# A first load in halves, and divisions and spreads moved to later slots, in a kernel of two attentions

## The chip, the cores and the metric

The kernel runs on one core of a Trainium2 chip. The metric is the device time in microseconds (us) of one execution. The core has five engines that run side by side, each through its own stream of instructions in order: PE (matrix products), DVE (element-wise work), ACT (functions such as exp, and copies), POOL (masks) and SP, which here issues every DMA. They wait for one another only through semaphores. Products land in PSUM banks; everything else lies in SBUF or in DRAM.

## The reference

Two attentions over 2048 tokens, width 640, 32 heads of 20, on their own inputs and weights; the outputs are put side by side. A is causal attention within chunks of 512 tokens, mixed by a gate with a read from a memory that the earlier chunks have filled. B is causal attention over a sliding window of 256 tokens.

```
# A, for each chunk s of 4
p = softmax(qs @ ks.T * scale + causal)
num, den = phi(qs) @ M, phi(qs) @ z + 1e-6       # phi(t) = t + 1 if t > 0 else exp(t)
o = g * num / den + (1 - g) * (p @ vs)           # g = sigmoid(beta), one per head
M, z = M + phi(ks).T @ vs, z + phi(ks).sum()
# B
p = softmax(where(0 <= i - j < 256, q @ k.T * scale, -1e9))
o = p @ v
# both
out = o @ wo
```

## The kernel before

The work is cut into eight phases, B and A in turn for chunks 0 to 3 of 512 tokens. A phase has eight units of four heads. The score blocks of a phase are packed, so that a pack fills 512 columns for each of four heads; phases have 20 packs (B's first and all of A's) or 24. A pack is a **slot**: 172 slots in all, numbered from 0. In a slot, `body` (lines 656 to 717) issues in this order:

1. whatever an earlier slot has put off to the start of this one (`self.after`, filled by `at`);
2. `scores` of the pack (line 451): the score products on PE, then two exponentials on ACT (line 465, each over two heads) and masks on POOL (lines 479 and 485);
3. what was put off to follow the scores (`self.behind`, filled by `at_end`), such as the parts of phi;
4. `weigh` of a unit whose exponentials are two slots old (line 495): the weighted sums on PE, a cast to the tile `oc` on DVE (line 527), and a DMA transpose to the tile `ocT` (line 529);
5. `prefetch`: turns of finished token tiles (DMA transposes to `oT`, line 571), as long as fewer than three are open;
6. projections, updates and reads of A's memory, and output products, chosen by `pick` from lists with estimated costs.

A unit's sums carry the sum of its weights as one more column. `normalise` (lines 540 to 564) divides: a reciprocal (line 544) and a product (line 549) on DVE, out of `ocT` into the token tile `ot`; where it is the last unit of a chunk of A other than the first and last, it also adds the memory's read (line 561). `weigh` puts `normalise` off by four slots (three in A's last chunk). When a chunk's eighth unit is divided, its four token tiles are ready to be turned and multiplied by the output weights (`out_half`, line 574).

The queries and keys of chunk 0 of B are projected straight into the layout that the scores need, four heads at partitions 0, 32, 64 and 96 (`proj_padded`, line 237). All others go through `proj` (line 261): the product is cast to a tile `qk` (line 270), written to a DRAM scratch `qd` or `kd` (line 271), and read back from there by `spread` (line 280) into `qp` and `kp`, in four DMAs, one for each place of a head. `proj` puts a spread off by two slots; it waits in SP's stream until the writes have landed, with everything that is queued on SP behind it.

PSUM has three two-bank tiles named `Sc`, for the scores, and two one-bank tiles named `D`, for all other products; a `D` tile is free again when DVE (or ACT) has copied it out. PE's stream is in order, so a product without a free `D` tile holds back all scores behind it.

The start: one DMA loads the first 512 tokens of B into a tile that bears the name `omem` (line 125), ahead of the weights on SP. Ten products of a zero tile run meanwhile on PE (line 210). Then `first_x` turns the tokens on PE, 20 transposes of 128x128 for five slices of the width (line 216), two slices to a `Sc` tile, and copies each slice to `xTB`, on DVE for the even slices (line 219) and on ACT for the odd ones (line 221).

Of the kernel before, what the change touches and what calls it, by code (L numbers as in the profile page):

```python
# [9 lines left out]
BF16 = mybir.dt.bfloat16  # L10
F32 = mybir.dt.float32

P = 128
S = 2048
D = 640
# [4 lines left out]
KT = 5  # L20
NC = 4
CH = 512
CT = CH // P
# [59 lines left out]
class Kern:  # L83
# [21 lines left out]
    def load_x(self, br, c):  # L105
        t = self.io.tile([P, KT, CH], BF16, name="xT" + br, bufs=1)
        self.nc.sync.dma_start_transpose(out=t[:], in_=self.x[br][c * CH:(c + 1) * CH, :])
        self.xT[br] = t

    def load_w(self, name, ap, eng, pad=0, halves=None):  # L110
        n = ap.shape[1]
# [7 lines left out]
    def setup(self):  # L119
        nc, cp, ins = self.nc, self.cp, self.ins  # L120
        wB = ins["B_wqkv"]
        self.w, self.wt = {}, {}
        brow = cp.tile([P, H], BF16, name="brow")
        xs = self.io.tile([P, CT, D], BF16, name="omem", bufs=1)
        nc.sync.dma_start(out=xs[:], in_=self.x["B"][0:CH, :].rearrange("(t p) d -> p t d", p=P))
        wk, wq = wB[:, D:2 * D], wB[:, 0:D]
        self.load_w("Bk", wk, nc.sync, 32, 0)
        self.load_w("Bq", wq, nc.sync, 32, 0)
        self.load_w("Bk", wk, nc.sync, 32, 1)
        self.load_w("Bq", wq, nc.sync, 32, 1)  # L130
        self.load_w("Bv", wB[:, 2 * D:3 * D], nc.sync)
        nc.sync.dma_start(out=brow[:], in_=ins["A_beta"].partition_broadcast(P))
        self.load_x("A", 0)
        self.load_w("Ak", ins["A_wk"], nc.sync)
        self.load_w("Aq", ins["A_wq"], nc.sync)
        self.load_w("Av", ins["A_wv"], nc.sync)
        self.load_w("Bo", ins["B_wo"], nc.sync)
        self.load_w("Ao", ins["A_wo"], nc.sync)

        z = self.wk.tile([P, CH], BF16, name="oc", bufs=2)  # L140
        nc.vector.memset(z[:], 0.0)
        one = cp.tile([P, 1], F32, name="one")
# [25 lines left out]
        self.v, self.vt = vs, vt  # L168
        self.first_x(xs, z)

        bm = cp.tile([P, KT, 8], F32, name="bmask")
        nc.gpsimd.memset(bm[:], 1.0)
        for m in range(KT):
            off = P * m - DH * (P * m // DH)
            nc.gpsimd.affine_select(out=bm[:, m, :], in_=bm[:, m, :], pattern=[[-DH, 8]],
                                    compare_op=ALU.is_ge, fill=0.0, base=off,
                                    channel_multiplier=1)
            nc.gpsimd.affine_select(out=bm[:, m, :], in_=bm[:, m, :], pattern=[[DH, 8]],
                                    compare_op=ALU.is_ge, fill=0.0, base=DH - 1 - off,
                                    channel_multiplier=-1)  # L180
        self.bm = bm
        self.macc = cp.tile([P, KT, 8, DH + 1], F32, name="macc")
        self.gate(brow)
# [20 lines left out]
    def first_x(self, xs, z):  # L204

        nc = self.nc
        for _ in range(2):
            ps = self.dtile([P, CH], F32)
            for i in range(5):
                nc.tensor.matmul(ps[:], lhsT=z[:, 0:P], rhs=z[:], start=(i == 0), stop=(i == 4))  # L210
        t = self.io.tile([P, KT, CH], BF16, name="xTB", bufs=1)
        for kt in range(KT):
            if kt % 2 == 0:
                ps = self.ps.tile([P, 2, 2 * CH], BF16, name="Sc", bufs=3)
            for tt in range(CT):
                nc.tensor.transpose(out=ps[:, kt % 2, tt * P:(tt + 1) * P],
                                    in_=xs[:, tt, kt * P:(kt + 1) * P], identity=self.ident[:])
            if kt % 2 == 0:
                nc.vector.tensor_copy(out=t[:, kt, :], in_=ps[:, 0, 0:CH])
            else:  # L220
                nc.scalar.copy(out=t[:, kt, :], in_=ps[:, 1, 0:CH])
        self.xT["B"] = t

# [13 lines left out]
    def proj_padded(self, which, g):  # L237

        nc = self.nc
        if g == 0:  # L240
            t = self.io.tile([P, G, CH], BF16, name="%spB" % which,
                             bufs=2 if which == "k" else 1)
            if which == "q":
                self.qp["B"] = t
            else:
                self.kp["B", 0] = t
        t = self.qp["B"] if which == "q" else self.kp["B", 0]
        ps = self.dtile([P, CH], F32)
        w = self.wt["B" + which]
        for kt in range(KT):  # L250
            for j in range(4):
                c0 = kt * D + DH * (4 * g + j)
                nc.tensor.matmul(ps[32 * j:32 * j + 32, :], lhsT=w[:, c0:c0 + 32],  # L253
                                 rhs=self.xT["B"][:, kt, :], start=(kt == 0),
                                 stop=(kt == KT - 1), tile_position=(0, 32 * j))
        if g == 0 and which == "q":
            nc.scalar.copy(out=t[:, g, :], in_=ps[:])
        else:
            nc.vector.tensor_copy(out=t[:, g, :], in_=ps[:])

    def proj(self, br, c, which, m, st):
        nc = self.nc
        if m == 0:
            st[which] = self.dram.tile([KT * P, CH], BF16, name="%sd%s" % (which, br), bufs=2)
        ps = self.dtile([P, CH], F32)
        for kt in range(KT):
            nc.tensor.matmul(ps[:], lhsT=self.w[br + which][:, kt, m * P:(m + 1) * P],  # L267
                             rhs=self.xT[br][:, kt, :], start=(kt == 0), stop=(kt == KT - 1))
        t = self.wk.tile([P, CH], BF16, name="qk", bufs=4)
        nc.vector.tensor_copy(out=t[:], in_=ps[:])  # L270
        nc.sync.dma_start(out=st[which][m * P:(m + 1) * P, :], in_=t[:])
        cut = {1: (0, 3), 3: (3, 6), 4: (6, 8)} if (br, c) in (("A", 0), ("B", 1)) else {4: (0, 8)}
        if (br, c) == ("A", 1):
            cut = {2: (0, 4), 4: (4, 8)}
        if m in cut:
            self.at(self.slot + 2, lambda: self.spread(br, c, which, st, *cut[m]))
        if br == "A":
            self.phi(c, which, m, t, st)

# [42 lines left out]
    def vproj(self, br, c, tt, hf):  # L322
        nc = self.nc
        ps = self.dtile([P, CH], F32)
        for kt in range(KT):
            nc.tensor.matmul(ps[:, 0:320], lhsT=self.xT[br][:, kt, tt * P:(tt + 1) * P],  # L326
                             rhs=self.w[br + "v"][:, kt, hf * 320:(hf + 1) * 320],
                             start=(kt == 0), stop=(kt == KT - 1))
        src = ps[:, 0:320].rearrange("p (h e) -> p h e", e=DH)
# [3 lines left out]
        else:  # L333
            nc.vector.tensor_tensor(  # L334
                out=self.v["A"][0][:, tt, hs, 0:DH], in0=src,
# [159 lines left out]
    def weigh(self, u):  # L495
        nc = self.nc
# [13 lines left out]
        for n, (kt, off, q0, nq, pt) in enumerate(jobs):  # L510
            v = self.vt[u.br][(kt // CT) % 2 if u.br == "B" else 0]
            for j in range(4):
                v0 = VW * (4 * u.g + j)
                nc.tensor.matmul(O[32 * j:32 * j + 32, q0 * P:(q0 + nq) * P],  # L514
                                 lhsT=v[:, kt % CT, v0:v0 + 32],
                                 rhs=pt[:, j, off * P:(off + nq) * P],
# [10 lines left out]
        nc.vector.tensor_copy(out=oc[:], in_=O[:])  # L527
        tp = self.wk.tile([P, CT, P], BF16, name="ocT", bufs=4)
        nc.sync.dma_start_transpose(out=tp[:], in_=oc[:])
        late = 3 if u.br == "A" and u.c == NC - 1 else 4  # L530
        self.at(self.slot + late, lambda: self.normalise(u, tp))

    def turn_here(self, u, oc):
# [285 lines left out]
```

## Time and profile before

| | us |
|---|---|
| median of three runs | 392.62 |
| lowest and highest run | 392.05, 395.66 |
| the profiled execution, as timed | 390.19 |
| its span in the profile | 388.1 |

| engine | busy us | share of the span | instructions |
|---|---|---|---|
| PE | 340.4 | 88% | 4060 |
| ACT | 338.1 | 87% | 384 |
| DVE | 276.7 | 71% | 581 |
| POOL | 251.8 | 65% | 392 |

The span runs from the first to the last instruction that the profile shows; 2.1 us of the time lie outside it. The granted clock of PE was 0.991 of full speed on average. The exponentials of line 465 are 320.7 of ACT's busy time, 344 of them.

Rows of a timeline give, in this order, the start in us from the span's start, the time taken, the engine, the line, the operation, the tile written and the tile read, and how many instructions are merged in the row; in brackets stands how long the engine was idle before it, and what ended that. SPq is SP's queue of DMA issues: its times are those of issuing, and the data land later. The trace also has an event for each landing. Rows of waits give who waited for whom, the total in us, how many times, and the longest.

### The profile page before, as it was taken

What the parts mean: (1) busy time and instruction counts of PE and PEld (TensorE: products, weight loads), DVE (VectorE), ACT (ScalarE), POOL (GpSimd) and SP (SyncE); (2) the same over time, 40 slices, a digit from 0 to 9 for tenths busy, and PEclk for the clock granted to TensorE, in tenths of its full rate; (3) what the DMA queues carried; (4) which work ended last, traced back from release to release, by engine and by line L of the source; (5) the groups of instructions that cost most, each with busy time, mean ns of one, the idle gap of its engine ahead of it and who ended that gap; (6) DMA issues with size and microseconds to landing.
All of it is one profiled execution on the core that took longest, in us unless ns stands there. A gap on an engine that the chain in (4) does not pass through costs nothing.

```text
span 388.1 us, 10554 instructions
## 1 busy us (share of the span) xinstructions
PE 340.4 (88%) x4060; PEld 161.3 (42%) x4060; DVE 276.7 (71%) x581; ACT 338.1 (87%) x384; POOL 251.8 (65%) x392
## 2 busy tenths in 40 slices
PE   7999988977998798988997989898999989988884
PEld 3433434322443344444543335444454435544442
DVE  2467667634788868788778886789877887777583
ACT  2867789985999889888999999988999999999972
POOL 9657564542777587635578888844458988955550
PEclk9999999998999989999999999999999999999999
DMA  8993328647434597728575697758474377736312
GB/s 256 314 285 77 47 83 151 113 105 187 134 80 134 143 173 141 135 71 137 117 135 135 127 190 126 149 104 110 116 146 120 92 169 129 113 78 113 96 30 70
DMA packets 110738, 50.77 MB, mean 131 GB/s; under 512 B 81760, under 2 KB 110688, under 8 KB 110688
## 3 DMA queue, kind: packets, MB, share of 16 engines
q1 hardware_dynamic: 110688, 50.10, 61.1%
q8 instruction: 32, 0.52, 0.6%
q14 instruction: 18, 0.15, 0.1%
HBM read 16.39 MB, written 14.42 MB: 79 GB/s over the span
## 4 chain that ended last, share of the span: by engine, by line
PE 42%; ACT 24%; DVE 16%; issue 6%; POOL 6%; DMA 3%; SPq 0%; POOLq 0%; DVEq 0%; ACTq 0%
ACT pt L465 22%; PE D L267 13%; PE Sc L459 7%; PE D L326 6%; PE D L580 5%; PE D L514 5%; PE D L253 4%; POOL pt L479 3%; DVE qk L270 3%; POOL pt L485 3%; DVE oc L527 3%; ACT pe L310 2%; PE Sc L628 2%; DVE omem L445 1%; DMA ocT<-oc 1%
## 5 line engine op out<-in xcount | busy, mean ns | idle before, releaser
L465 ACT ACTIVATE pt<-Sc 128x1024 bf16<-128x1024 f32 (+1 forms) x344 | 320.7, 1077 | 32.3 <-PE Sc L459 28.2
L479 POOL TENSOR_SCALAR_AFFINE_SELECT pt<-pt 128x512 bf16<-128x512 bf16 x254 | 167.6, 671 | 117.2 <-ACT pt L465 116.9
L485 POOL TENSOR_SCALAR_AFFINE_SELECT pt<-pt 128x512 bf16<-128x512 bf16 x112 | 78.6, 717 | 5.1 <-ACT pt L465 4.8
L270 DVE CAST qk<-D 128x512 bf16<-128x512 f32 x70 | 47.9, 687 | 29.4 <-PE D L267 26.8
L527 DVE CAST oc<-D 128x512 bf16<-128x512 f32 x62 | 42.7, 688 | 19.9 <-PE D L514 19.8
L459 PE MATMUL Sc<-qpB,kpB 20*128 20x256 bf16 (+2 forms) x704 | 43.3, 277 | 7.8 <-ACT pt L465 4.7
L459 PE MATMUL Sc<-qpA,kpA 20*128 20x384 bf16 (+3 forms) x512 | 41.0, 302 | 5.8 <-ACT pt L465 5.0
L580 PEld LDWEIGHTS <-oT 128*128 128x128 bf16 x280 | 25.4, 98 | 17.9 <-issue 6.6
L583 DVE CAST ot<-D 128x320 bf16<-128x320 f32 x56 | 27.0, 485 | 7.2 <-PE D L580 6.4
L459 PEld LDWEIGHTS <-kpB 20*128 20x128 bf16 x704 | 13.6, 92 | 42.5 <-issue 38.5
L267 PE MATMUL D<-xTA,Aq 128*128 128x512 bf16 x100 | 24.9, 379 | 4.6 <-DVE oc L527 3.5
L326 PE MATMUL D<-Av,xTA 128*128 128x320 bf16 x160 | 26.2, 300 | 2.8 <-DVE vA L334 1.6
L514 PE MATMUL D<-pt,vA 128*32 128x256 bf16 (+3 forms) x576 | 23.5, 287 | 5.7 <-DVE qk L270 2.2
L580 PE MATMUL D<-Bo,oT 128*128 128x320 bf16 x160 | 27.3, 306 | 1.0 <-DVE omem L445 0.4
L267 PE MATMUL D<-xTA,Ak 128*128 128x512 bf16 x100 | 25.3, 384 | 2.1 <-DVE qk L270 2.0
L326 PE MATMUL D<-Bv,xTB 128*128 128x320 bf16 x160 | 26.0, 300 | 1.4 <-DVE oc L527 0.9
L514 PE MATMUL D<-pt,vB 128*32 128x384 bf16 (+2 forms) x720 | 26.1, 277 | 0.5 <-DVE qk L270 0.3
L459 PEld LDWEIGHTS <-kpA 20*128 20x128 bf16 x512 | 11.7, 91 | 30.6 <-issue 27.9
L267 PE MATMUL D<-xTB,Bq 128*128 128x512 bf16 x75 | 19.8, 396 | 3.4 <-DVE qk L270 3.2
L549 DVE TENSOR_TENSOR otB<-ocT,rr 128x320 bf16<-128x320 bf16 x32 | 20.2, 631 | 1.1
L544 DVE RECIPROCAL rr<-ocT 128x16 f32<-128x16 bf16 x62 | 15.1, 243 | 8.0 <-DMA ocT<-oc 8.0
L580 PE MATMUL D<-Ao,oT 128*128 128x320 bf16 x120 | 20.1, 299 | 0.7 <-DVE qk L270 0.4
(84 smaller groups left out, 358.8 us busy)
## 6 DMA issues: line engine op xcount, KB each, us to landing
out_dram<-ot SPq DMA_DIRECT2D x31, 160.0 KB
kdA<-qk SPq DMA_DIRECT2D x20, 128.0 KB
qdA<-qk SPq DMA_DIRECT2D x20, 128.0 KB
kdB<-qk SPq DMA_DIRECT2D x15, 128.0 KB
qdB<-qk SPq DMA_DIRECT2D x15, 128.0 KB
kpB<-kdB SPq DMA_DIRECT2D x8, 160.0 KB
qpB<-qdB SPq DMA_DIRECT2D x8, 160.0 KB
kpA<-kdA SPq DMA_DIRECT2D x8, 160.0 KB
```

Of the source, the lines that this page charges most:

```text
L267: nc.tensor.matmul(ps[:], lhsT=self.w[br + which][:, kt, m * P:(m + 1) * P], rhs=self.xT[br][:, kt, :], start=(kt == 0), stop=(kt == KT - 1))
L270: nc.vector.tensor_copy(out=t[:], in_=ps[:])
L326: nc.tensor.matmul(ps[:, 0:320], lhsT=self.xT[br][:, kt, tt * P:(tt + 1) * P], rhs=self.w[br + "v"][:, kt, hf * 320:(hf + 1) * 320], start ...
L459: nc.tensor.matmul(ps[j // 2][:, j % 2, off * P:(off + nq) * P], lhsT=kp[rows, u.g, k0:k0 + P], rhs=self.qp[u.br][rows, u.g, q0 * P:(q0 + ...
L465: nc.scalar.activation(out=pt[:, 2 * hp:2 * hp + 2, 0:pk.used], in_=ps[hp][:, :, 0:pk.used], func=ACT.Exp, scale=SCALE)
L479: nc.gpsimd.affine_select(out=blk, in_=blk, pattern=[[0, 4], [1, P]], compare_op=ALU.is_ge, fill=0.0, base=0, channel_multiplier=-1)
L485: nc.gpsimd.affine_select(out=blk, in_=blk, pattern=[[0, 4], [-1, P]], compare_op=ALU.is_ge, fill=0.0, base=-1, channel_multiplier=1)
L514: nc.tensor.matmul(O[32 * j:32 * j + 32, q0 * P:(q0 + nq) * P], lhsT=v[:, kt % CT, v0:v0 + 32], rhs=pt[:, j, off * P:(off + nq) * P], star ...
L527: nc.vector.tensor_copy(out=oc[:], in_=O[:])
L549: nc.vector.tensor_tensor(out=o[:, :, cols].rearrange("p b (j e) -> p b j e", j=4), in0=pv[:, :, :, 0:DH], in1=rr[:].unsqueeze(3).to_broad ...
L580: nc.tensor.matmul(ps[:, 0:320], lhsT=st["oT"][:, m, :], rhs=self.w[br + "o"][:, m, hf * 320:(hf + 1) * 320], start=(m == 0), stop=(m == K ...
L583: nc.vector.tensor_copy(out=st["ot"][:, hf * 320:(hf + 1) * 320], in_=ps[:, 0:320])
```

## The change

Five things are different. Slices of the turned tokens are now a list, so that they may lie in two tiles. The first 512 tokens of B come in two DMAs of 256 tokens each, into tiles that bear the names `otA` and `otB`. There are seven products of zeros in place of ten, and the five turned slices go to five PSUM tiles of their own (three `Sc`, two `D`); all transposes of the first half stand ahead of those of the second, and a slice is copied after its second half, the odd ones into a tile that bears the name `phiq`. The spreads of chunks 2 and 3 are put off by three slots in place of two. `normalise` is put off by six slots in chunks 0 and 1 and by five in chunks 2 and 3, in place of four; A's last chunk keeps its three.

```diff
@@ load_x
-        self.xT[br] = t
+        self.xT[br] = [t[:, kt, :] for kt in range(KT)]
@@ setup
-        xs = self.io.tile([P, CT, D], BF16, name="omem", bufs=1)
-        nc.sync.dma_start(out=xs[:], in_=self.x["B"][0:CH, :].rearrange("(t p) d -> p t d", p=P))
+        xs = [self.io.tile([P, CT, D], BF16, name="ot" + br, bufs=2) for br in "AB"]
+        for i in range(2):
+            nc.sync.dma_start(out=xs[i][:, 0:2, :], in_=self.x["B"][256 * i:256 * i + 256, :]
+                              .rearrange("(t p) d -> p t d", p=P))
@@ first_x
-        for _ in range(2):
+        for n in (4, 3):
             ps = self.dtile([P, CH], F32)
-            for i in range(5):
-                nc.tensor.matmul(ps[:], lhsT=z[:, 0:P], rhs=z[:], start=(i == 0), stop=(i == 4))
-        t = self.io.tile([P, KT, CH], BF16, name="xTB", bufs=1)
-        for kt in range(KT):
-            if kt % 2 == 0:
-                ps = self.ps.tile([P, 2, 2 * CH], BF16, name="Sc", bufs=3)
-            for tt in range(CT):
-                nc.tensor.transpose(out=ps[:, kt % 2, tt * P:(tt + 1) * P],
-                                    in_=xs[:, tt, kt * P:(kt + 1) * P], identity=self.ident[:])
-            if kt % 2 == 0:
-                nc.vector.tensor_copy(out=t[:, kt, :], in_=ps[:, 0, 0:CH])
-            else:
-                nc.scalar.copy(out=t[:, kt, :], in_=ps[:, 1, 0:CH])
-        self.xT["B"] = t
+            for i in range(n):
+                nc.tensor.matmul(ps[:], lhsT=z[:, 0:P], rhs=z[:], start=(i == 0), stop=(i == n - 1))
+        ps = [self.ps.tile([P, 4 * CH], BF16, name="Sc", bufs=3) for _ in range(3)]
+        ps += [self.dtile([P, 2 * CH], BF16) for _ in range(2)]
+        t = [self.io.tile([P, KT, CH], BF16, name=n, bufs=1) for n in ("xTB", "phiq")]
+        self.xT["B"] = [t[kt % 2][:, kt, :] for kt in range(KT)]
+        for i in range(2):
+            for kt in range(KT):
+                for tt in range(2):
+                    c0 = (2 * i + tt) * P
+                    nc.tensor.transpose(out=ps[kt][:, c0:c0 + P],
+                                        in_=xs[i][:, tt, kt * P:(kt + 1) * P],
+                                        identity=self.ident[:])
+                if i and kt % 2 == 0:
+                    nc.vector.tensor_copy(out=self.xT["B"][kt], in_=ps[kt][:, 0:CH])
+                elif i:
+                    nc.scalar.copy(out=self.xT["B"][kt], in_=ps[kt][:, 0:CH])
@@ proj
-            self.at(self.slot + 2, lambda: self.spread(br, c, which, st, *cut[m]))
+            self.at(self.slot + (3 if c > 1 else 2), lambda: self.spread(br, c, which, st, *cut[m]))
@@ weigh
-        late = 3 if u.br == "A" and u.c == NC - 1 else 4
+        late = 3 if u.br == "A" and u.c == NC - 1 else 6 if u.c < 2 else 5
```

Left out are the places in `proj_padded`, `proj` and `vproj` that take a slice from the list in place of the tile. In `proj`, `c` is the chunk that is projected, one ahead of the phase's own.

More of the change, by code (lines that the diff above doesn't have):

```diff
@@ L253, in proj_padded @@
                 nc.tensor.matmul(ps[32 * j:32 * j + 32, :], lhsT=w[:, c0:c0 + 32],
-                                 rhs=self.xT["B"][:, kt, :], start=(kt == 0),
+                                 rhs=self.xT["B"][kt], start=(kt == 0),
                                  stop=(kt == KT - 1), tile_position=(0, 32 * j))
@@ L267, in proj @@
             nc.tensor.matmul(ps[:], lhsT=self.w[br + which][:, kt, m * P:(m + 1) * P],
[L268 removed]
+                             rhs=self.xT[br][kt], start=(kt == 0), stop=(kt == KT - 1))
         t = self.wk.tile([P, CH], BF16, name="qk", bufs=4)
@@ L325, in vproj @@
         for kt in range(KT):
-            nc.tensor.matmul(ps[:, 0:320], lhsT=self.xT[br][:, kt, tt * P:(tt + 1) * P],
+            nc.tensor.matmul(ps[:, 0:320], lhsT=self.xT[br][kt][:, tt * P:(tt + 1) * P],
                              rhs=self.w[br + "v"][:, kt, hf * 320:(hf + 1) * 320],
```

## Prediction

> **What bounds the kernel now.** I read the page first, then the waits, then the timelines of ACT, DVE and SP's queue, and last the chain of waits at the start and around 100 us. The page says that ACT (338.1 us of 388.1) and PE (340.4) are both busy for most of the span. The program runs in 172 slots, each with two exponentials of line 465 on ACT; counting those rows in pairs gives each slot's start. Where nothing else interferes a slot takes 1.81 us, and 1.81 us is two such exponentials, so there ACT is the bound. The rest is lost where ACT waits:
>
> ```profile
> ACT pt L465 <- PE Sc L459: 28.2, 36, 3.9
> DVE rr L544 <- DMA ocT<-oc: 8.0, 6, 3.3
> ```
>
> These are totals, times and the longest. The second row is the wait the change aims at: a division (line 544) that stands in DVE's stream before its turned tile ocT has landed. The two longest of its six, and what ACT did beside them:
>
> ```profile
> 79.77 0.25 DVE L544 RECIPROCAL rr<-ocT 128x16 f32<-128x16 bf16 x1 [2.74 <-DMA ocT<-oc]
> ...
> 87.97 0.25 DVE L544 RECIPROCAL rr<-ocT 128x16 f32<-128x16 bf16 x1 [3.31 <-DMA ocT<-oc]
> ```
>
> ```profile
> 71.59 9.44 ACT L465 ACTIVATE pt<-Sc 128x1024 bf16<-128x1024 f32 x10
> 82.87 5.61 ACT L465 ACTIVATE pt<-Sc 128x1024 bf16<-128x1024 f32 x6 [1.84 <-PE Sc L459]
> 92.38 2.85 ACT L465 ACTIVATE pt<-Sc 128x1024 bf16<-128x1024 f32 x3 [3.91 <-PE Sc L459]
> ```
>
> DVE stands still, no D bank is emptied, PE stops, and ACT idles 1.84 + 3.91 = 5.75 us (slots 32 and 35). Why is ocT late? SP's queue there is an almost solid row of issues from 56.99 to 96.15; a few of its rows:
>
> ```profile
> 71.72 3.84 SPq L571 DMA_TRANSPOSE oT<-otB  x3
> 76.09 1.14 SPq L271 DMA_DIRECT2D kdA<-qk  x1
> 77.34 1.20 SPq L529 DMA_TRANSPOSE ocT<-oc  x1
> 79.29 1.41 SPq L291 DMA_DIRECT2D kpA<-kdA  x4
> ...
> 83.99 1.41 SPq L291 DMA_DIRECT2D qpA<-qdA  x4
> 85.50 2.50 SPq L529 DMA_TRANSPOSE ocT<-oc  x2
> ...
> 97.45 1.42 SPq L291 DMA_DIRECT2D qpB<-qdB  x4
> ```
>
> The ocT issued at 77.34 was ready in oc at 70.4 (cast 69.72 + 0.69): SP is some 7 us behind the engines. That matters for what follows, because SP also carries the next phase's q (qpB, 97.45), which slot 40 needs.
>
> **The change, part by part.** The after kernel keeps every projection, score, weighted sum and output product in its slot. What moves: the division two slots later in chunks 0 and 1, one later in chunks 2 and 3 (A's last chunk unchanged); the turns (line 571) that hang on a finished tile: B0's first three from slot 25 to 27, A0's first from 46 to 47, B3's first from 157 to 158; spreads of chunks 2 and 3 one slot later; and the start.
>
> *Start.* The chain there is one load, then turning in shared tiles:
>
> ```profile
> 0.80 4.26 DMA omem<-in_B_x_dram
> 5.11 0.41 PE Sc L216 x4
> 5.54 0.43 DVE xTB L219
> ...
> 7.14 0.61 PE Sc L216 x8
> 7.75 2.30 PE D L253 x40
> ```
>
> From landing (5.06) to the first projection takes 2.62 us (the timeline puts it at 7.68), because PE waits for a copy before reusing each shared tile. After: the first half lands earlier and its 10 transposes (10 x 0.076, from 8 in 0.61) run before the second lands. The second half ends the same bytes in the same queue; it lands between 5.06 and 5.57 (one more issue, 0.49 to 0.51), I take 5.2. Then ACT, which must empty the bank that the first projection takes over, copies at 5.2 + 0.05 + 4 x 0.076 + 0.05 = 5.6 and needs 2 x 0.58 = 1.16, to 6.8; DVE's three copies (3 x 0.42 + gaps) end at 6.75. The projection starts at 6.8 in place of 7.68: -0.9. Its weights landed at 6.54 by the trace's landing events, so they still cover this. The PE has three matmuls less to warm up: the rows of line 210 step by 0.43 us until 3.79 and faster after, so seven end near 4.25, and ten transposes follow at once. Bounds: -1.0 (landing at 5.06) and +0.3 (landing at 5.57 and 20 transposes at double their 0.076 plus a projection stretched by 0.6). Nothing holds the gain up behind it: the next weights, Bv, land at 12.20 and are wanted at 13.70 - 0.9.
>
> The Trainium skill, "TensorE: Matmul & The Clock Gate", Part 1, speaks against this edit: the warm-up is about 3.4 us of activity, not a number of matmuls. This trace's cadence turned faster about 2.9 us after the first matmul, so the rule's window is near what seven matmuls fill. By the rule alone, a window that closes too late would leave the first products at half rate and cut this gain to about nothing.
>
> *Division later, slots 28 to 47.* DVE's work is the same (0.24 + 0.49 per unit, a common 0.73 us), only later in its stream. The waits of 2.74 and 3.31 go: with the three turns (3.84 us of issue) behind, kdA goes out at 71.7, the first late ocT at 72.3, landing near 74.8 (2.41 to 2.48 in all rows of its kind), and its division is two slots later. The second late ocT stays behind the turns and qpA in SP's queue, to be issued at 83.9 to 85.5 and to land by 88; its division now stands in slot 35, which unstalled starts at 79.03 + 4 x 1.81 = 86.3, so up to 1.5 us of wait may stay. At best 5.75 us return by slot 36.
>
> What is late next: slot 40's scores. They need qpB, whose last piece landed at 100.68; PE took it up at
>
> ```profile
> 101.12 0.40 PE L459 MATMUL Sc<-qpB,kpB 20*128 20x384 bf16 x8
> ```
>
> a mere 0.44 us later. All of SP's issues before it are still to be made, in the same number, so relieving DVE alone advances slot 40 by 0.4. SP itself gets faster only by its waits: 0.52 (75.56 to 76.09), 0.74 (78.54 to 79.29, for kdA to land), 1.37 (82.62 to 83.99, for qdA) and 1.30 (96.15 to 97.45, for qdB), and by kdA's issue of 1.14 against 0.35 elsewhere. Some of that is chance: the landing of qdB took 3.77 us where its kind takes 1.7 to 1.9, and the third turn 4.30 against 2.6; an instruction fetch of 16 KB ran in the DMA queues beside each, at 94.66 and 75.63. PE reaches the second of those points about 5 us earlier relative to SP after the change, where nothing urgent is in flight. If both go, qpB lands at 97.8 and slot 40 advances by 3.3. Bounds -0.4 and -3.3; I take -2.2, nearer to the good end for that reason. Later slots here are bound by PE and DVE with as many divisions in them as before: 0, within 0.7 either way.
>
> *Division and spreads later, chunks 2 and 3.* The remaining waits of line 544 are 0.17, 0.65 and 0.90 us at 230.17, 242.11 and 332.21. ACT ran past them (its timeline has 56 exponentials of line 465 without an idle row from 324.04 for 51.49 us, and 20 from 234.19), so they are worth 0; ACT is the cover, and without it they would be 1.7. The spreads pass one or two ocT or qd writes in SP's queue. Where a spread is tight (qpB for slot 84 landed at 197.17, wanted at 197.98), its order against SP's other issues does not change, as no SP work stands between slots 79 and 80: 0, and +0.5 at worst from the 7 us that kpB's four transfers (177.36 to 184.39) now take later. The long add of 1.80 us (line 561, 209.72) moves with its unit; it stalls PE 2.01 us now and will stall it in slot 91 about as much: 0, within 0.8.
>
> *B3's first turn.* At slot 158 it stands behind the ocT of the weighted sum of that slot on SP (now issued 351.67; about 350.95 once DVE's 0.7 moves), so it goes out near 352.2 and lands 2.6 later, 354.8. Its product in slot 160 came up on PE at 353.26. PE then waits 1.5 us, slot 161's scores queue behind it, and ACT, at 354.98 now, starts near 355.9: +0.9. Bounds 0 and +1.9 (issued at 352.95 as B3's second turn is now, 355.60). I take +0.8. From there to the tail ACT runs at its own pace, so it isn't won back.
>
> Sum: -0.9 - 2.2 + 0.8 = -2.3 us. Against the profiled execution (390.19, of which 388.14 span) that is 387.9; the median of the runs shown is 392.62, so 390.3.
>
> **Rivals.** *All of the stall comes back.* If SP's waits shrink enough that qpB is there when slot 40 comes (96.3 unstalled), then -0.9 - 5.75, with no loss at B3's turn: 386.0. For it: four waits and a slow issue sum to 4.7 us. Against it: SP's row is otherwise solid, and two of its waits are a write's own 1.7 to 1.9 us to land. *Slower through B3's turn.* The turn lands at 355.60, ACT loses 1.9; start gains nothing and slot 40 only 0.4: 392.62 + 1.5 = 394.1. It decides from the point at which the turn's loss passes the two gains together, 1.3 us at the least of them. For it: the order on SP is fixed and its ocT waits for DVE. Against: it needs both other terms at their poor ends. *The change only moves the waits.* DVE waits at slot 35 for the ocT behind the turns, slot 40 for qpB, B3's turn eats the start: 0 to -1, 392.1.
>
> **How the numbers follow.** About 1% (3.9 us) is what a measurement can tell from no change. Forecast (-1 to -3.9): 0.45. Full return (-4 to -7): 0.31. Waits only moved: 0.14. Slower: 0.10. Faster by over 1% is the second case and 0.02 of the first, 0.33; slower by over 1% needs the fourth together with poor ends of the small terms (0.5 + 0.8 + 0.7), 0.06; the rest, 0.61, is within. The predicted time is the forecast's, 390.3. The range runs from the full return, 386.2, to the slower rival, 394.1.
>
> **What would show it.** Right: the first projection on PE near 6.8; no wait of line 544 over 1.6 us before 100 us; ACT's long idle moved from slots 32 and 35 to slot 40, with PE waiting there for qpB; a new wait on oT in slot 160. Wrong: no wait at slot 40 (then the gain is near 6 us), or DVE's wait back at slot 35 at its old size; or a first projection after 7.7.

## The result and the profile after

The changed kernel takes 405.34 us (median of four runs, 402.83 to 405.8), beside 393.01 for the kernel before (four runs, 392.05 to 395.66): a ratio of 1.030, 95% interval 1.026 to 1.035. It is slower by 12 us; the forecast was 390.3, and no rival of it reached further than 394.1. Here and below the medians are over all executions, while the ratios leave out those more than 1.5% above the fastest of their kernel, so that a ratio need not be the quotient of the two medians. The profiled execution took 405.8 us, of which 403.9 are its span, 15.8 more than that of before. The lines of the code are five further down than in the kernel before (the exponentials are line 470, the reciprocal of the division 549, the cast to `oc` 532, the cast to `qk` 275).

The wait that the change aimed at is gone: the list of waits has no row in which the reciprocal waits for a DMA. In its place, totals, times and the longest:

```profile
ACT pt L470 <- PE Sc L464: 40.2, 42, 4.2
...
DVE qk L275 <- DMA kdB<-qk: 4.7, 1, 4.7
...
DVE oc L532 <- DMA ocT<-oc: 3.3, 1, 3.3
```

ACT waits 40.2 us for scores where it waited 28.2, and DVE has two new waits for DMAs, 8.0 us together, as much as the six that went. ACT's timeline says when:

```profile
75.30 14.97 ACT L470 ACTIVATE pt<-Sc 128x1024 bf16<-128x1024 f32 x16
91.81 3.77 ACT L470 ACTIVATE pt<-Sc 128x1024 bf16<-128x1024 f32 x4 [1.53 <-PE Sc L464]
99.83 1.94 ACT L470 ACTIVATE pt<-Sc 128x1024 bf16<-128x1024 f32 x2 [4.24 <-PE Sc L464]
102.37 1.94 ACT L470 ACTIVATE pt<-Sc 128x1024 bf16<-128x1024 f32 x2 [0.61 <-PE Sc L464]
```

Slots 32 and 35 now pass without a stop (they are in the first row), and slots 36 and 38 stop for 1.53 and 4.24 us. The timelines of DVE and PE at that place:

```profile
89.40 0.69 DVE L532 CAST oc<-D 128x512 bf16<-128x512 f32 x1 [3.29 <-DMA ocT<-oc]
...
96.13 0.69 DVE L275 CAST qk<-D 128x512 bf16<-128x512 f32 x1 [4.74 <-DMA kdB<-qk]
```

```profile
90.14 1.24 PE L272 MATMUL D<-xTB,Bk 128*128 128x512 bf16 x5 [1.60 <-DVE oc L532]
...
96.87 2.29 PE L272 MATMUL D<-xTB,Bq 128*128 128x512 bf16 x5 [3.38 <-DVE qk L275]
...
104.06 0.40 PE L464 MATMUL Sc<-qpB,kpB 20*128 20x384 bf16 x8
```

`oc` has two buffers and `qk` four. A cast into either needs the DMA that reads its old content to be done, and these DMAs stand far back in SP's queue: by the order of the casts and the writes, the write that the second of the two casts waits for was issued at 92.31, for a cast that began at 82.32. So DVE, no longer held by a division, is held by the next thing that hangs on SP. Slot 40, whose scores are the last row, is 2.9 us later than before rather than earlier; 1.7 of that was there by slot 20 (see below).

To place the whole loss, each slot's start is taken from its first exponential on ACT, and the kernel before is taken off. The differences of the profiled executions, by stage, in us (worked out from the timelines; a row adds up to the difference of the spans, but for rounding):

| kernel | to slot 20 | 20-40 | 40-72 | 72-113 | 113-135 | 135-140 | 140-171 | end |
|---|---|---|---|---|---|---|---|---|
| changed kernel | 1.7 | 1.2 | 3.2 | 1.7 | 2.5 | 1.8 | 2.2 | 1.5 |
| start alone | 0.0 | -0.1 | 0.3 | 0.0 | 0.1 | 0.3 | 0.0 | 1.7 |
| divisions alone | 1.8 | -0.1 | 3.2 | 1.3 | 2.6 | 1.5 | 0.9 | -0.1 |
| divisions, chunks 0 and 1 | 2.0 | 0.2 | 3.2 | 0.9 | 0.1 | 0.0 | 0.5 | 1.3 |
| divisions, chunks 2 and 3 | 2.3 | 0.3 | 0.2 | 0.3 | 1.0 | 1.5 | 2.2 | 1.4 |
| two passes, 6 and 5 slots | 1.9 | 0.0 | 3.2 | -0.1 | 0.3 | 1.5 | 1.2 | 0.0 |
| two passes, 7 and 6 slots | 0.0 | 0.0 | 0.1 | -0.1 | -0.3 | 1.5 | 1.8 | 0.0 |
| chunk 0 alone | 1.8 | 0.0 | 2.0 | 1.3 | 0.1 | 0.0 | 0.0 | 0.0 |
| later, apart | 0.0 | 0.8 | 0.5 | 1.9 | -0.3 | 1.5 | 0.0 | 0.0 |
| chunk 0, load later | 0.0 | -3.5 | 0.7 | 0.0 | 0.1 | 0.0 | 0.0 | 0.0 |
| changed, mended | 0.0 | -3.4 | 0.5 | 1.3 | 0.1 | 0.3 | 0.0 | 2.7 |

Several columns need care. A step of 1.3 to 1.7 us at slot 19 comes in ten of the eighteen profiles of this study, that of before among the other eight, and in kernels with and without the later divisions. It goes with PE's granted clock, here in the changed kernel and then, for comparison, in the kernel before (columns: the stretch, its length, busy time of PE, PEld, DVE, ACT and POOL with counts, PE's clock, share of the DMA engines, GB/s):

```profile
50.63:54.04 3.41, 1.81 (x23) 0.68 (x21) 1.45 (x3) 2.20 (x3) 1.34 (x3) 1.00 0.40 107
54.04:57.46 3.42, 3.42 (x16) 0.99 (x17) 1.19 (x2) 1.57 (x2) 2.81 (x5) 0.50 0.12 42
88.17:91.59 3.42, 1.82 (x17) 0.60 (x13) 1.95 (x4) 2.10 (x3) 1.85 (x3) 1.00 0.54 113
91.59:101.83 10.24, 6.86 (x50) 2.15 (x42) 2.63 (x5) 5.71 (x6) 2.44 (x4) 0.50 0.72 187
```

```profile
79.13:82.55 3.42, 1.79 (x25) 0.62 (x14) 1.93 (x5) 1.90 (x3) 1.85 (x3) 1.00 0.34 85
82.55:85.96 3.41, 3.41 (x30) 1.19 (x22) 1.29 (x2) 3.09 (x4) 1.02 (x2) 1.00 0.26 77
```

In the changed kernel two stretches of 3.41 us in which PE was busy for only half are followed by one or more in which its clock is 0.50; in the kernel before, one just as empty is not, so a half-empty stretch alone does not decide it. These stretches follow a grid: the first three of half clock in the changed kernel start at 54.04, 91.59 and 139.4, 11 and 14 times 3.41 us apart. The grid lies differently in each execution, so the same gap can be caught in one run and missed in another. The end column is of the same kind: it is 1.3 to 2.7 where a whole stretch of half clock falls on the tail, in kernels with and without the later divisions. Slots 140 to 171 hold half clock too: the 1.2 and 1.8 of the two passes, which leave B's last chunk alone, stand in part beside half clock at slots 158 and 159. By its mean clock of 0.951 the changed kernel spends some 40 us at half clock (0.049 of 403.9, doubled), the kernel before, at 0.991, some 7. How much of the 12 us passes through the clock is not separated by these runs as a whole; where two kernels share a step and only one has the half clock, it is said below.

### The profile page after: what moved, and what is told of

The parts are those of the page before. It is cut to its first block, busy times and chain, and to the rows that moved or that the text cites. A ratio compares the mean times of both kernels' runs of the same rounds, so it can differ in the third digit from the quotient of the medians.

```text
span 403.9 us, 10576 instructions
## 1 busy us (share of the span) xinstructions
PE 351.6 (87%) x4057; PEld 164.6 (41%) x4057; DVE 272.4 (67%) x581; ACT 339.0 (84%) x384; POOL 249.9 (62%) x392
## 4 chain that ended last, share of the span: by engine, by line
PE 46%; DVE 20%; ACT 17%; DMA 7%; issue 6%; POOL 2%; SPq 2%; ACTq 0%; DVEq 0%; POOLq 0%
PE D L272 16%; ACT pt L470 15%; PE Sc L464 7%; PE D L585 6%; PE D L331 5%; PE D L519 5%; DVE qk L275 4%; PE D L258 4%; DVE oc L532 3%; ACT pe L315 2%; DVE otA L554 2%; DMA qpB<-qdB 2%; PE Sc L633 2%; DMA Bk<-in_B_wqkv_dram 1%; DVE omem L450 1%
## 5 line engine op out<-in xcount | busy, mean ns | idle before, releaser
L470 ACT ACTIVATE pt<-Sc 128x1024 bf16<-128x1024 f32 (+1 forms) x344 | 321.3, 1064 | 45.3 <-PE Sc L464 40.2
L464 PE MATMUL Sc<-qpB,kpB 20*128 20x256 bf16 (+2 forms) x704 | 45.2, 279 | 9.5 <-ACT pt L470 6.3
L272 PE MATMUL D<-xTA,Aq 128*128 128x512 bf16 x100 | 27.2, 406 | 6.3 <-DVE oc L532 6.3
L585 PE MATMUL D<-Bo,oT 128*128 128x320 bf16 x160 | 28.2, 312 | 2.7 <-DMA oT<-otB 1.7
L519 PE MATMUL D<-pt,vA 128*32 128x256 bf16 (+3 forms) x576 | 25.4, 306 | 3.2 <-DVE qk L275 1.8
L272 PE MATMUL D<-xTA,Ak 128*128 128x512 bf16 x100 | 26.4, 396 | 0.3 <-DVE qk L275 0.2
L272 PE MATMUL D<-xTB,Bq 128*128 128x512 bf16 x75 | 20.8, 413 | 4.3 <-DVE qk L275 4.1
L272 PE MATMUL D<-xTB,Bk 128*128 128x512 bf16 x75 | 20.9, 414 | 2.4 <-DVE oc L532 1.6
L339 DVE TENSOR_TENSOR vA<-D,omg 128x320 bf16<-128x320 f32 x32 | 15.3, 486 | 7.2 <-PE D L331 6.8
```

The lines of the kernel that those rows point to most:

```text
L464: nc.tensor.matmul(ps[j // 2][:, j % 2, off * P:(off + nq) * P], lhsT=kp[rows, u.g, k0:k0 + P], rhs=self.qp[u.br][rows, u.g, q0 * P:(q0 + ...
L470: nc.scalar.activation(out=pt[:, 2 * hp:2 * hp + 2, 0:pk.used], in_=ps[hp][:, :, 0:pk.used], func=ACT.Exp, scale=SCALE)
L585: nc.tensor.matmul(ps[:, 0:320], lhsT=st["oT"][:, m, :], rhs=self.w[br + "o"][:, m, hf * 320:(hf + 1) * 320], start=(m == 0), stop=(m == K ...
```

## The experiments

**Which part.** The start alone, the divisions alone, and the divisions of chunks 0 and 1 or 2 and 3 alone, then the spreads alone. All are the kernel before with one part of the change.

Start alone: the hunks of `load_x`, `setup` and `first_x`, and those that read the slices.

> Only the start of the change (two half loads, five tiles of their own, seven zero products); divisions and spreads as before. Theory 1 (the later divisions cost the time: DVE's wait on ocT goes over into waits of the casts for oc and qk, PE stands still longer at a stretch, and windows of half clock on PE follow): within 0.5% of before, 391 to 395 us, and the half-clock windows before 110 us stay at one or two. Theory 2 (the start costs it: the weights land later, PE is warm later, and all that follows is shifted against the windows in which the clock is granted): 400 us or more, with eight or so half-clock windows as in the changed kernel.

Measured: 392.84 beside 392.34; ratio 1.001 (0.997 to 1.005).

Divisions alone:

```diff
-        late = 3 if u.br == "A" and u.c == NC - 1 else 4
+        late = 3 if u.br == "A" and u.c == NC - 1 else 6 if u.c < 2 else 5
```

> Only the later divisions (six slots in chunks 0 and 1, five in 2 and 3), with the old start and the old spreads. Theory 1: most of the loss, 400 to 406 us, DVE waiting over 3 us for qk or oc near 90 us and three windows of half clock in a row there. Theory 2: no loss, 388 to 394 us.

Measured: 403.93; ratio 1.029 (1.022 to 1.036).

Chunks 0 and 1 alone (`else 6 if u.c < 2 else 4`):

> Only the divisions of chunks 0 and 1 later (six slots), all else as before. Theory 1: the part of the loss that arises before about 200 us, +3 to +7 us, so 396 to 400. Theory 2: 388 to 394 us.

Measured: 398.14; ratio 1.013 (1.007 to 1.019).

Chunks 2 and 3 alone (`else 4 if u.c < 2 else 5`):

> Only the divisions of chunks 2 and 3 later (five slots), all else as before. Theory 1: a loss of 3 to 6 us after 200 us, the turn of B's last chunk in slot 160 among it (1 to 2 us and a window of half clock behind it). Theory 2: 391 to 394 us.

Measured: 397.21; ratio 1.010 (1.002 to 1.018).

Spreads alone:

```diff
-            self.at(self.slot + 2, lambda: self.spread(br, c, which, st, *cut[m]))
+            self.at(self.slot + (3 if c > 1 else 2), lambda: self.spread(br, c, which, st, *cut[m]))
```

> Only the third part of the change: spreads of chunks 2 and 3 one slot later. All theories: same as before within 1%, 391 to 394, since the spread tiles are wanted many slots later.

Measured: 393.91 beside 392.24; ratio 1.002 (0.998 to 1.007).

What follows: the later divisions are the loss, in both halves; start and spreads are neither gain nor loss. But in the table most of chunk 1's loss stands in slots 48 to 72, where nothing had waited for a division before. What those slots have new is a matter of arithmetic. B's units are weighed every 3 slots there, so a division 4 slots after its unit falls between two weighed units and one 6 slots after falls into the very slot of another. A's units come every 2.5 slots: 4 or 6 fall between, 5 always meets. So the change, with 6 in B's chunk 1 and 5 in A's chunk 2, hits the two bad cases. Going through the code's schedule, 18 more divisions share a slot with a weighted sum in the changed kernel than in the kernel before, where only A's last chunk has any. A division is issued at the start of its slot, ahead of the weighted sum, so DVE takes it first and empties the bank of the sum 0.73 us later. This was the new theory, and it was put against plain lateness.

**Meeting or lateness.** The same two passes, once with the meeting values and once later still but apart:

```diff
-        late = 3 if u.br == "A" and u.c == NC - 1 else 4
+        late = {"B1": (6, 6, 6, 6, 6, 6, 6, 6), "A2": (5, 5, 5, 5, 5, 5, 5, 5), "A3": (3, 3, 3, 3, 3, 3, 3, 3)}.get(u.br + str(u.c), (4, 4, 4, 4, 4, 4, 4, 4))[u.g]
```

> Only two passes changed against before: B's chunk 1 with its divisions 6 slots after their unit in place of 4, A's chunk 2 with 5 in place of 4. Both values put nearly every division of the pass (14 of 16) into a slot in which the next unit's weighted sum is also issued; before has none of those. Theory 1 (meeting): a division issued ahead of a weighted sum stands on DVE in front of the cast of its bank to oc, PE waits for that bank: PE's waits for the cast of oc in slots 113 to 134 rise as in the run with the late divisions in chunks 2 and 3 alone (single waits from below 0.4 to 0.5 to 0.9 us), slots 48 to 71 and 116 to 135 lose 2.5 to 6 us together, time 395 to 399. Theory 2 (lateness): a division costs by being later, wherever it falls: the same 395 to 399 here, and at least as much in the run with 7 and 6 slots. Theory 3 (neither; the loss of the change sits around slots 28 to 47 and at B's last chunk): 391.5 to 393.5.

```diff
-        late = 3 if u.br == "A" and u.c == NC - 1 else 4
+        late = {"B1": (7, 7, 7, 7, 7, 7, 7, 6), "A2": (6, 6, 6, 6, 6, 6, 6, 5), "A3": (3, 3, 3, 3, 3, 3, 3, 3)}.get(u.br + str(u.c), (4, 4, 4, 4, 4, 4, 4, 4))[u.g]
```

> The same two passes as in the run with 6 and 5 slots, one slot later still: B's chunk 1 with 7 (its last unit 6), A's chunk 2 with 6 (its last unit 5). Now no division falls into a slot with a weighted sum. Theory 1 (meeting): no cost, 391.5 to 393.5, although every one of these divisions is later than in the other run. Theory 2 (lateness): as much as with 6 and 5 or more, 395 to 400. Theory 3 (neither): 391.5 to 393.5, as for the other run.

Measured beside 393.43: 398.08 with 6 and 5 (ratio 1.018, 1.011 to 1.025), 393.26 with 7 and 6 (1.005, 1.000 to 1.010). The later kernel is the faster one, so plain lateness falls for these passes. Slots 40 to 72 lose 3.2 us with 6, 0.1 with 7; 0.9 of the 3.2 comes in slots 70 and 71, beside half clock. The same products on PE, in slots 65 to 69, first where they meet:

```profile
164.34 0.36 PE L435 MATMUL D<-mz,phiq 128*128 128x147 bf16 x5 [0.91 <-DVE oc L527]
...
171.64 0.36 PE L435 MATMUL D<-mz,phiq 128*128 128x84 bf16 x5 [0.91 <-DVE oc L527]
172.54 2.32 PE L267 MATMUL D<-xTB,Bk 128*128 128x512 bf16 x5 [0.21 <-DVE omem L445]
```

and where they are apart:

```profile
160.92 0.36 PE L435 MATMUL D<-mz,phiq 128*128 128x147 bf16 x5 [0.36 <-DVE oc L527]
...
167.57 0.36 PE L435 MATMUL D<-mz,phiq 128*128 128x84 bf16 x5 [0.25 <-DVE oc L527]
168.47 1.25 PE L267 MATMUL D<-xTB,Bk 128*128 128x512 bf16 x5 [0.21 <-DVE omem L445]
```

PE waits 0.91 us for the bank in place of 0.36 and 0.25. DVE's timeline in the first kernel shows what stands ahead of the cast:

```profile
162.91 0.24 DVE L544 RECIPROCAL rr<-ocT 128x16 f32<-128x16 bf16 x1
163.19 0.49 DVE L549 TENSOR_TENSOR otB<-ocT,rr 128x320 bf16<-128x320 bf16 x1
163.60 0.68 DVE L527 CAST oc<-D 128x512 bf16<-128x512 f32 x1
```

And each longer gap of PE can lose twice: the projection behind the second one runs its five products in 2.32 us against 1.25, at half clock. The changed kernel has the same pair:

```profile
172.66 0.36 PE L440 MATMUL D<-mz,phiq 128*128 128x84 bf16 x5 [0.91 <-DVE oc L532]
173.55 2.32 PE L272 MATMUL D<-xTB,Bk 128*128 128x512 bf16 x5 [0.21 <-DVE omem L450]
```

For A's chunk 2 the waits came as expected (0.84 and 0.55 us for the cast of `oc`, which the two theories share), but the time did not: slots 113 to 135 lost 0.3 there, against 2.5 in the changed kernel, where a half clock followed. With the divisions of chunks 2 and 3 alone, which has the same divisions there and no half clock in those slots, they lost 1.0. That part of the expectation, 14 meetings of about equal price, was too simple.

**Chunk 0 and SP.** Only chunk 0's divisions later, none of them meeting:

```diff
-        late = 3 if u.br == "A" and u.c == NC - 1 else 4
+        late = {"B0": (6, 6, 6, 6, 6, 6, 6, 6), "A0": (6, 6, 6, 6, 6, 6, 6, 4), "A3": (3, 3, 3, 3, 3, 3, 3, 3)}.get(u.br + str(u.c), (4, 4, 4, 4, 4, 4, 4, 4))[u.g]
```

> Only chunk 0 changed: the divisions of B's and A's chunk 0 6 slots after their unit (A's last unit 4), so that none meets a weighted sum. Theory 1: the stalls of slots 32 and 35 go (5 to 6 us), and 4 to 7 us come back in slots 36 to 40 as waits for the casts of oc and qk, whose buffers are held by transfers queued on SP: net -1 to +1.5, time 391 to 394. The rival, that the loss comes from this region, gives 395 to 398 by slot 48 already.

Measured: 396.04 beside 393.43; ratio 1.014 (1.002 to 1.026), in total within the rival's range. By slot it isn't: slots 32 and 35 gain 1.7 and 3.9, slots 36 to 40 lose 5.8, and the stage 20 to 40 ends at 0.0. Of the 5.1 us that its profiled execution is longer, 1.8 are there by slot 20, and 0.8 come at slot 47; the rest, near slots 56 and 91, stands where its clock is at 0.50. The total alone would have misled. The waits for DMAs between 60 and 104 us:

```profile
DVE qk L270 <- DMA kdB<-qk: 4.6, 1, 4.6
DVE oc L527 <- DMA ocT<-oc: 2.4, 1, 2.4
```

If SP is what bounds there, taking work from SP must bring a gain. The next kernel is the same with the load of A's next tokens put behind B's projections:

```diff
-                 + self.a_v("A", 0, 1, 14) + self.a_x("A", 1) + B[:8],
+                 + self.a_v("A", 0, 1, 14) + B[:8] + self.a_x("A", 1),
```

> As the run with only chunk 0's divisions 6 slots late, and the transposing load of A's chunk 1 (2.6 to 2.9 us of SP, wanted in slot 47) is issued in slot 39 in place of 31; the spread of q for the next phase moves from slot 41 to 40. Theory (SP is the bound): the wait for the cast of qk in slots 36 to 38 (4.6 us) shrinks by about the 2.7 us that SP no longer spends ahead of the write it waits for; slot 40 1.5 to 3 us earlier than in that run, 391 to 393.5 if nothing behind slot 40 becomes late. Rival: no change in slots 36 to 40, 394 to 397.

Measured: 392.61 beside 392.24; ratio 0.994 (0.988 to 1.000). The medians show no gain in total; the stage does. Its profiled execution, the second fastest of ten at 387.38, has slot 40 3.5 us earlier than before, and between 60 and 104 us the long wait for `kdB<-qk` is gone:

```profile
DVE oc L527 <- DMA ocT<-oc: 3.0, 1, 3.0
PE Sc L459 <- DMA qpA<-qdA: 0.2, 1, 0.2
```

The other relief leaves the load and moves the writes:

```diff
-        nc.sync.dma_start(out=st[which][m * P:(m + 1) * P, :], in_=t[:])
+        eng = nc.gpsimd if 20 <= self.slot < 40 else nc.sync
+        eng.dma_start(out=st[which][m * P:(m + 1) * P, :], in_=t[:])
```

with chunk 0's divisions late as above:

> As the run with only chunk 0's divisions 6 slots late, and in slots 20 to 39 the writes of the projected q and k to DRAM are issued by POOL in place of SP (some 14 of them, 0.4 to 0.6 us of SP each). Theory (SP is the bound of slots 28 to 40, so a stall that is taken away at a division comes back at the next thing that waits for SP): with about 8 us less on SP the waits for the casts of qk and oc in slots 36 to 39 go too; slot 40 starts 4 to 6 us earlier than in before, time 386 to 390. Rival (the waits of slots 36 to 39 come from somewhere else, the clock or DVE): slot 40 as in the run with chunk 0's divisions alone, 393 to 397. Unknown: what an issue costs on POOL, whose masks PE waits for; if each takes over 1 us there, single slots lose 0.5 to 1 us and half of the gain goes.

and with the divisions of before:

> Before with that one edit alone: in slots 20 to 39 POOL issues the writes of q and k. Divisions as before. Theory (SP is the bound there): the turned tiles ocT land in time for divisions 4 slots late too, the waits of 2.74 and 3.31 us go or shrink below 1 us each, and so do those for qk: slot 40 starts 4 to 6 us earlier, time 386 to 390. Rival (divisions must be later for the stalls to go): above 391.

Measured beside 392.24: 390.51 (ratio 0.995, 0.990 to 1.000) and 389.02 (0.994, 0.989 to 0.999). The stage 20 to 40 gains 3.2 and 3.9 us. An issue on POOL is a row of about half a microsecond there:

```profile
84.50 0.56 POOL L272 DMA_DIRECT2D kdB<-qk  x1 [0.31 <-DVE qk L270]
```

So both reliefs show SP as the bound of slots 28 to 40, though the gain of POOL's issues stayed below the 4 to 6 us expected, and with the divisions of before two waits of the reciprocal stayed, 3.5 us in all, where each was expected below 1. With POOL issuing the writes, the later divisions bring nothing more: the kernel that leaves them at 4 gains as much. The moved load without later divisions, and both reliefs together:

> Before with that load moved and nothing else; divisions 4 slots late as before. The ocT whose landing the two long waits of slots 32 and 35 are for are issued ahead of where the load stood, so these waits stay (5.5 us); behind them SP is no longer late. If the later divisions of chunk 0 are needed for the gain: slot 40 within 2 us of before, 391 to 393. If the load alone is the gain: slot 40 3 us earlier or more, 387 to 390.

> Before with both reliefs of SP: in slots 20 to 39 POOL issues the writes of q and k, and the load of A's chunk 1 goes out in slot 39; divisions as before. Waits of 1.5 to 2 us for ocT stay in slots 32 and 35, as with POOL's writes alone; the rest of slots 36 to 40 is free: slot 40 2 to 4 us earlier than before, 387 to 390. The meetings theory asks for no later division here.

Measured beside 393.14: 393.44 for the load alone (ratio 0.999, 0.995 to 1.002; its waits of the reciprocal for `ocT` stayed, 5.4 us, the longest 2.8) and 387.95 for both (0.988, 0.983 to 0.993). So the moved load is another matter than POOL's issues: alone it gains 0.5 us in slots 20 to 40, with chunk 0's divisions later 3.5; there the two parts need each other. The kernel with both reliefs is faster than both kernels of this study, with no division moved; it is the one gain here of more than 1%.

**All later, but apart; and the changed kernel mended.** First the kernel before with every division later and none meeting:

```diff
-        late = 3 if u.br == "A" and u.c == NC - 1 else 4
+        late = {"B0": (6, 6, 6, 6, 6, 6, 6, 6), "A0": (6, 6, 6, 6, 6, 6, 6, 4), "B1": (5, 5, 5, 5, 5, 5, 5, 6), "A1": (6, 6, 6, 6, 6, 6, 6, 4), "B2": (5, 5, 5, 5, 5, 5, 5, 4), "A2": (6, 6, 6, 6, 6, 6, 6, 5), "B3": (5, 5, 5, 5, 5, 5, 5, 4), "A3": (3, 3, 3, 3, 3, 3, 3, 3)}.get(u.br + str(u.c), (4, 4, 4, 4, 4, 4, 4, 4))[u.g]
```

> Every division later than before, as in the change or nearly so, but each kept out of the slots with a weighted sum: B 6, 5, 5, 5 slots in chunks 0 to 3, A 6, 6, 6, 3, last units at 4 to 6; B's last division of chunk 3 stays at 4, so the first turn of that chunk stays in slot 157. The start and the spreads are those of before. Theory 1 (meeting, and the first turn of B's last chunk one slot late): nearly all of the 11 us that the later divisions cost goes, 391 to 395; slots 48 to 135 and 161 to 163 show no loss. Theory 2 (lateness): 399 to 405.

Measured: 397.03 beside 393.43 (ratio 1.015, 1.007 to 1.022; profiled at 394.56). Half of the loss went, not nearly all: a miss between the two theories. The table has what was left: nothing in slots 140 to 171, where the first turn of B's last chunk kept its slot; 0.8 in slots 20 to 40 (SP); 1.9 in slots 72 to 113, where this kernel divides two units in slot 89, just ahead of the long add, but where its clock also is at 0.50 for a stretch, so that the two can't be told apart; and 1.5 in slots 135 to 140. That last step, 1.5 to 1.8, is in all seven kernels whose last division of A's chunk 2 comes later than slot 133, and it is at most 0.3 in the others (0.6 of it was gained in the slot before, so it is 0.9 to 1.2 net). There the add of 1.80 us stands at another place in DVE's order; no run moved it alone. In the changed kernel, DVE and then PE:

```profile
314.05 1.80 DVE L566 TENSOR_TENSOR otA<-otA,omem 128x2560 bf16<-128x2560 bf16 x1
315.77 0.68 DVE L275 CAST qk<-D 128x512 bf16<-128x512 f32 x1
```

```profile
316.50 0.84 PE L519 MATMUL D<-pt,vB 128*32 128x384 bf16 x24 [1.42 <-DVE qk L275]
```

PE waited 0.41 us behind that add before:

```profile
303.59 0.84 PE L580 MATMUL D<-Ao,oT 128*128 128x320 bf16 x5 [0.41 <-DVE qk L270]
```

Then the changed kernel itself with only the load moved, and with the load moved and these lates:

```diff
-        late = 3 if u.br == "A" and u.c == NC - 1 else 6 if u.c < 2 else 5
+        late = {"B0": (6, 6, 6, 6, 6, 6, 6, 6), "A0": (6, 6, 6, 6, 6, 6, 6, 4), "B1": (5, 5, 5, 5, 5, 5, 5, 6), "B2": (5, 5, 5, 5, 5, 5, 5, 4), "B3": (5, 5, 5, 5, 5, 5, 5, 4), "A3": (3, 3, 3, 3, 3, 3, 3, 3)}.get(u.br + str(u.c), (4, 4, 4, 4, 4, 4, 4, 4))[u.g]
```

> The changed kernel with one edit: the load of A's chunk 1 issued in slot 39 in place of 31, so that SP comes 2.7 us earlier to the writes and the q that slots 36 to 40 wait for. SP part alone: 3 to 4.5 us less by slot 40, 400.5 to 402.5 in all; the meetings' loss behind slot 48 stays as it was.

> The changed kernel with its start and its spreads, and its divisions still later (B 6, 5, 5, 5 slots in chunks 0 to 3, A's chunk 0 6, A's chunks 1 and 2 back at 4), but none added to a slot with a weighted sum, the first turn of B's last chunk back in slot 157, and the load of A's chunk 1 issued in slot 39 in place of 31. If meeting, that turn and SP's queue are the whole loss: 389 to 394, 11 to 16 below the changed kernel. If something else of the change costs too: 397 or more.

Measured beside 393.14: 400.01 (ratio 1.020, 1.013 to 1.027) and 391.56 (0.996, 0.992 to 1.000). Against the 1.030 of the changed kernel, the load gives back 1.0% and the lates another 2.4%: together the whole loss. What is left of the change, its start, its spreads and B's later divisions, costs nothing that these runs can measure. These lates also put A's chunks 1 and 2 back to four slots, so for A they do not tell meeting from lateness.

## Why the prediction was wrong

*Start, -0.9: nothing.* The turning came out near the forecast, but not as forecast: the halves had landed by 4.60 us by the landing events, earlier than the 5.2 assumed, but the transposes ran slower, starting 0.107 us apart where they started 0.055 apart before. That is the half rate which the prediction named as a danger beside this term, seen by the spacing alone (the clock column reads 1.00 there). The last copies ended at 6.94 and 7.02 in place of 6.75 and 6.8.

```profile
5.28 0.85 PE L221 MATMUL Sc<-ident,otB 128*128 128x128 bf16 x6
```

Then the step "its weights landed at 6.54 by the trace's landing events, so they still cover this" failed, and with it the term. The weights' DMA stands one issue further back, and its landing is the first piece of the chain that ended last:

```profile
1.82 5.99 DMA Bk<-in_B_wqkv_dram
7.85 2.42 PE D L258 x40
```

It landed at 7.81, and PE waited 1.37 us for it; the first projection came at 7.85 in place of 7.68. The bound of +0.3 held this; the value was taken at the wrong end, from a landing of the old kernel that the edit itself had moved. In one execution (the changed kernel with the load moved) PE waited 2.10 us there, and its clock went to 0.50 from 8.2 to 11.6 us: slot 0 came 1.9 late. There the half rate came by way of the weights.

*The stall of slots 32 and 35: right that it goes, wrong in what is next.* Both stops went, 5.75 us, with no reciprocal waiting for `ocT`. The list of what is late next had only one entry, slot 40's `qpB`. The nearer ones were DVE's own next casts: `qk`, with four buffers whose writes stood behind the load in SP's queue, and `oc`, with two. The term (-2.2, bounds -0.4 and -3.3) came out at +1.2 in the changed kernel and between -0.1 and 0.8 in the four kernels that divide chunk 0 later on the old start, with SP's work as before. The general argument beside it was right and should have been carried through: SP's issues remain as many, so relieving DVE alone advances nothing.

*"Later slots here are bound by PE and DVE with as many divisions in them as before: 0, within 0.7 either way": the step that failed most.* The number of divisions in a stretch was the same, their place in DVE's order was not. Slots 40 to 72 lost 3.2 us of it in the changed kernel, and 3.2 against 0.1 in the two passes, where meeting or not is the difference (0.9 of it beside half clock). The prediction did say that the kernel is bound by PE and DVE there; the row to look at was which DVE work stands ahead of a cast that frees a `D` bank.

*Chunks 2 and 3, 0 because ACT covers: wrong,* 2.5 us in slots 113 to 135 and 1.8 in 135 to 140. Of the 2.5, 1.0 is there with the divisions of chunks 2 and 3 alone; the other 1.5 comes at slot 116, beside a half clock. For the 1.0 the meetings are the likely cause, as PE's longer waits say, but with A's meetings alone the stage lost only 0.3. The cover was argued for the three waits that would vanish, and not for the new places of the divisions. The long add was said to stall PE about as much as before, within 0.8: for A's chunk 2 the cost was 0.9 to 1.2 net in all seven kernels that moved it, with PE waiting 1.42 us in place of 0.41. For A's chunk 1 (slot 91) it stays open; a step of 1.2 us is there also in kernels that didn't move it, beside a half clock.

*B3's first turn, +0.8 (0 to 1.9): right in mechanism and nearly in size.* It is issued and waited for as forecast:

```profile
364.19 2.55 SPq L576 DMA_TRANSPOSE oT<-otB  x2
```

```profile
366.87 0.85 PE L585 MATMUL D<-Bo,oT 128*128 128x320 bf16 x5 [1.73 <-DMA oT<-otB]
```

PE waits 1.73 us where 1.5 were forecast, and slot 161 is 1.1 later (0.9 forecast). The stage's 2.2 us have a second part that was not foreseen, 0.4 at slot 162 and 0.9 at slot 163, beside half clock from 368.1 to 374.9 us; the kernel with the divisions alone has 1.2 at slot 161, no half clock there, and no second step. Of the kernels in the table that leave that turn in slot 157, the stage is 0 in all that have no half clock in it.

*The spreads, 0:* right.

*The rivals.* That all comes back (386.0, for which the range has 386.2) and that waits only move (392.1) both took it for granted that nothing is lost behind slot 48. The slower rival had the right sign and one of the right mechanisms, at 1.5 us of 12. What no case held was a cost of the division's new place, and a part for PE's clock behind a new gap. Two of the prediction's own signs of being wrong came: the first projection at 7.85, and no wait at slot 40, though not with the gain that this was to mean.

## What to carry to other kernels

When work is put off by a number of slots, write down what it will stand next to there: in a loop with a period, one slot more or less decides whether it lands ahead of the copy that frees a bank or in a gap. When a wait is taken from an engine that waits for a late queue, list every later instruction of that engine that needs the same queue, buffers that are reused among them; if the queue is full, try taking work off it first: that gained 3.2 to 3.9 us of the stage here, and DVE's relief alone nothing. Take a landing time as a cover only if the edit leaves the transfers ahead of it alone.

## What the runs showed of the hardware

PE's clock fell to 0.50 for stretches of 3.41 us or multiples of it. One such drop came after a stretch in which PE was busy for 1.81 us of 3.41, with no gap over about 1 us (50 to 54 us of the changed kernel); PE need not be idle for a whole stretch. The Trainium skill, "TensorE: Matmul & The Clock Gate", Part 1, gives an idle window of about 3.4 us as what throttles; the window's length agrees with these rows, the idleness does not. The eighteen profiles, each laid on the grid of its own half clock (10 to 370 us, stretches at full clock), give counts and no sharp border: all 12 stretches with PE busy for under 40% were followed by half clock, 40 of 72 with 40 to 60%, and 15 of 1739 with more.

Whether a given gap is caught depends on where the grid lies in that execution: at slot 19 it cost 1.3 to 1.7 us in ten profiles of eighteen and nothing in the rest. Runs of one kernel lie up to 2% apart here, and the clock goes with it: of the ten executions of the kernel with chunk 0 late and the load moved, the two fastest (386.9 and 387.4 us) had a mean clock of 0.994 and 0.996, the five slowest (393.3 to 395.0) of 0.970 to 0.972.
